# Parallel attention and Mish block: the first root's tiles on two engines, a logarithm behind an eviction, query tiles begun behind scores, two selecting products as one

## Chip, cores and metric

The kernel runs on one core of one Trainium2 chip. The metric is the device time of one execution in microseconds; of several runs the median is given.

## What is computed

A pre-normalised transformer block whose attention and feed-forward halves stand side by side. B = 1, S = 2048 tokens, D = 512, H = 32 heads of Dh = 16, one key head and one value head for all query heads, F = 1792, all in float32:

```python
xn = layernorm(x)                                  # over D, eps = 1e-5
q  = (xn @ wq) as 32 heads;  k = xn @ wk;  v = xn @ wv
p  = softmax(q k^T * Dh ** -0.5)
A  = (p @ v, heads side by side) @ wo
h  = xn @ w1 + b1
Bf = (h * tanh(softplus(h))) @ w2                  # Mish
out = x + A + Bf
```

## The kernel before

Tokens are worked on in four chunks of 512 (`NC`, `CT`), each of four tiles of 128 (`NT`). Engines are called PE (TensorE), DVE (VectorE), ACT (ScalarE), POOL (GpSimd) and SP (DMA issue). The order on every engine is the order in which the code issues; there is no scheduler. Two functions put work off: `later(delay, stage, tag)` queues a step and `run_due` or `flush` issues it. Most products are split into a high and a low fp32r part, with three products in place of one.

There are three sections. The **opening** (to about 97 us) loads the tokens, normalises them, transposes them, forms keys, values and all query tiles, and takes the score maxima of the first unit of four heads. The **hand-ordered section** follows the string `PLAN`, one letter for one step (scores, maxima, exponentials, values, feed-forward products and so on). The **end**, `last_quotient`, divides the last two heads' sums and adds their share of the output projection.

*Normalising a chunk.* `statistics` (L325, L326) takes mean and variance. `rooted` puts variance and negative mean on DVE (L332, L333) and a logarithm and an exponential on ACT (L334, L335) as a first estimate of the reciprocal root. `root` improves it by one step, on POOL or DVE (L339 to L345). `normalise` (L351) applies mean and factor to a token tile on DVE or POOL; `normalise_on_two` leaves the tiles from `n` on to ACT (L359), for which DVE first multiplies factor and mean into a bias (L355). Chunk 0 goes in two halves: the root of tiles 0 and 1 on POOL, that of tiles 2 and 3 on DVE, after which `first_transposes` (L366, evicted by ACT at L368 and DVE at L392) waits for all four tiles. ACT also rounds weight blocks to their high part and POOL subtracts for the low part (`split`, L240, L241).

*Banks.* PSUM has eight banks. Six of them go round as three pairs, taken by `pair_bank` in turn for each step of first maxima (two scores, L495, emptied by one DVE reduction, L512) and for each transpose group of chunks 2 and 3 (L380, emptied by ACT at L382 and L387). While `beside` still holds transposes and key tiles, every query tile uses the same other bank, 7: its twelve products (L708) are followed by an eviction on ACT (L453, and L454 for the high part), and the next tile's first product waits for L453. The key products of a chunk are L417.

*The loop of first maxima.* Steps `i` = 0 to 31 each issue two scores and a reduction. Between them `beside_slot` issues a transpose group or three key products, and `fill_to_end(n)` up to `n` query products; a tile that ends early leaves the rest in `owed`, for the next call. At `i` = 1 the second half of the statistics of chunk 3 and its `rooted` are issued, then a whole query tile.

*The end.* `pick` holds columns of the identity that select, out of the 128 rows of the last value sums `ov`, the 64 sums of exponentials and the 64 weighted sums. Two products (L621, L622) put them in two banks, both at partitions 64 to 127. ACT takes logarithm and exponential of the former (L626, L627), DVE improves and multiplies (L628 to L630), ACT and DVE split the result (L633, L634), and `last_products` (L647) adds the last block of the output projection, for which 18 other products of L647 are the filler before it. L637 adds and L638 stores.

Of the kernel before, what the change touches and what calls it, by code (L numbers as in the profile page):

```python
# [12 lines left out]
ALU = mybir.AluOpType  # L13
# [7 lines left out]
NT = CT // P  # L21
# [157 lines left out]
def attention_and_mlp(ctx: ExitStack, tc: tile.TileContext, x, wq, wk, wv, wo, w1, b1, w2, out):  # L179
    nc = tc.nc  # L180
    E = mybir.EngineType
    PE, SP = nc.tensor, nc.sync
    ACT, DVE, POOL = nc.scalar, nc.vector, nc.gpsimd
# [12 lines left out]
    BANK = [banks[:, i] for i in range(8)]  # L196
# [8 lines left out]
    turn, beside = [0], [None]  # L205
# [32 lines left out]
    def split(hi, lo, src):  # L238

        ACT.activation(hi, src, AF.Copy)  # L240
        POOL.tensor_tensor(out=lo, in0=src, in1=hi.bitcast(F32), op=ALU.subtract)  # L241
# [86 lines left out]
    def rooted(c, some=slice(0, NT)):  # L328
        if c not in ROOT:
            ROOT[c] = [first.tile([P, NT], F32, tag=n, name=f"{n}{c}", bufs=2) for n in ("v", "y", "z", "m")]  # L330
        v, y, z, m = (t[:, some] for t in ROOT[c])
        DVE.tensor_scalar(v, MV[c][:, some, 1], EPS, -0.5, op0=ALU.add, op1=ALU.mult)  # L332
        DVE.tensor_scalar_mul(m, MV[c][:, some, 0], -1.0)  # L333
        ACT.activation(z, v, AF.Ln, scale=-2.0)  # L334
        ACT.activation(y, z, AF.Exp, scale=-0.5)  # L335

    def root(c, engine, some=slice(0, NT)):
        v, y, z, m = (t[:, some] for t in ROOT[c])
        engine.tensor_tensor(out=z, in0=y, in1=y, op=ALU.mult)  # L339
        engine.tensor_tensor(out=z, in0=z, in1=v, op=ALU.mult)  # L340
        if engine is DVE:
            DVE.scalar_tensor_tensor(out=y, in0=z, scalar=1.5, in1=y, op0=ALU.add, op1=ALU.mult)
        else:
            engine.tensor_scalar_add(z, z, 1.5)
            engine.tensor_tensor(out=y, in0=y, in1=z, op=ALU.mult)  # L345

    def normalise(c, engine, some=range(NT)):
        v, y, z, mean = ROOT[c]
        for t in some:
            x, m, r = XS[c, t], mean[:, t : t + 1], y[:, t : t + 1]  # L350
            engine.tensor_scalar(x, x, m, r, op0=ALU.add, op1=ALU.mult)  # L351

    def normalise_on_two(c, n, begin=0):
        v, y, z, mean = ROOT[c]
        DVE.tensor_tensor(out=z[:, n:], in0=y[:, n:], in1=mean[:, n:], op=ALU.mult)  # L355
        normalise(c, DVE, range(begin, n))
        for t in range(n, NT):
            x, b, r = XS[c, t], z[:, t : t + 1], y[:, t : t + 1]
            ACT.activation(x, x, AF.Identity, bias=b, scale=r)  # L359

    def first_transposes():
        xt, FLAT[0] = x_tile(0, work)
        pts = [pair_bank(f"xt0_{k}") for k in range(2)]
        for t in range(NT):
            for d in range(DT):
                PE.transpose(pts[d // 2][:, d % 2, t * P : (t + 1) * P], XS[0, t].rearrange("p (n d) -> p d n", d=DT)[:, d], ident)  # L366
        for d in range(DT):
            ACT.activation(xt[:, 0, d], pts[d // 2][:, d % 2], AF.Copy)  # L368
            if d % 2:
                hi, lo = (xt[:, k, d - 1 : d + 1] for k in range(2))  # L370
                later(0, lambda hi=hi, lo=lo, pt=pts[d // 2]: below(DVE, lo, pt, hi), ("lo", 0))
# [28 lines left out]
    XS, ST, MV, ROOT, FLAT = {}, {}, {}, {}, {}  # L400
# [211 lines left out]
    def last_quotient():  # L612

        c, mt = NC - 1, DT - 1
        rows = slice(64, P)
        pick = late_pool.tile([P, 2, HG * DH], F32, name="pick")
        DVE.tensor_copy(pick.rearrange("p k (h d) -> p k h d", h=HG), ident.rearrange("p (h k d) -> p k h d", h=HG, k=2))
        po, pd = (BANK[4 + k][rows] for k in range(2))
        ov = OV[(NU - 1) % 2]
        last_sums(0, 2)  # L620
        PE.matmul(pd, pick[:, 0], ov, start=True, stop=True)  # L621
        PE.matmul(po, pick[:, 1], ov, start=True, stop=True)  # L622
        last_sums(2, NT)
        hi, lo = (OHL[c, mt][rows, k] for k in range(2))
        o, d, r, z = oc[rows], dc[rows], r0[rows], z0[rows]
        ACT.activation(z, pd, AF.Ln)  # L626
        ACT.activation(r, z, AF.Exp, scale=-1.0)  # L627
        DVE.tensor_tensor(out=d, in0=pd, in1=r, op=ALU.mult)  # L628
        DVE.scalar_tensor_tensor(out=r, in0=d, scalar=2.0, in1=r, op0=ALU.subtract, op1=ALU.mult)
        DVE.scalar_tensor_tensor(out=o, in0=po, scalar=-1.0, in1=r, op0=ALU.mult, op1=ALU.mult)  # L630
        for t in range(NT):
            q = slice(t * P, (t + 1) * P)
            ACT.activation(hi[:, q], o[:, q], AF.Copy)  # L633
            DVE.tensor_tensor(out=lo[:, q], in0=o[:, q], in1=hi[:, q].bitcast(F32), op=ALU.subtract)  # L634
        for t in range(NT):
            last_products(t, mt)
            DVE.tensor_tensor(out=YS[t], in0=BANK[t], in1=YS[t], op=ALU.add)  # L637
            SP.dma_start(out=of[c * CT + t * P : c * CT + (t + 1) * P, :], in_=YS[t])  # L638

    def last_sums(t0, t1):  # L640
        for t in range(t0, t1):
            for mt in range(DT - 1):
                last_products(t, mt)

    def last_products(t, mt):
        for k, (i, j) in enumerate(TERMS):
            PE.matmul(  # L647
                BANK[t],
                OHL[NC - 1, mt][:, i, t * P : (t + 1) * P],
                RG[(blocks_of[NC - 1, "wo"] + mt) % RING][:, j],  # L650
                start=mt == 0 and k == 0,
                stop=mt == DT - 1 and k == 2,
            )
# [69 lines left out]
    done, left = [0], [0]  # L723
# [16 lines left out]
    with tc.tile_pool(name="first", bufs=1) as first:  # L740
# [36 lines left out]
        statistics(0, range(2))  # L777
        rooted(0, halves[0])
        root(0, POOL, halves[0])
        for r in (0, 64):  # L780
            hi, lo = (wkv[:, i, :, r : r + 48].rearrange("p t (k d) -> p t k d", k=3) for i in range(2))
            split(hi, lo, wkv_raw[:, :, None, :DH].to_broadcast([P, DT, 3, DH]))
        statistics(0, range(2, NT))
        rooted(0, halves[1])
        normalise(0, DVE, range(2))
        root(0, DVE, halves[1])
        normalise_on_two(0, 3, 2)
        for r in (0, 64):
            split(wkv[:, 0, :, r + 48 : r + 64], wkv[:, 1, :, r + 48 : r + 64], wkv_raw[:, :, DH:])
# [41 lines left out]
        def beside_slot():  # L831

            while beside:
                if next(beside[0], beside) is not beside:
                    return 3 if len(beside) % 2 else 2
                beside.pop(0)
            return 0

        owed = [0]

        def fill_to_end(n):
            n += owed[0]
            owed[0] = n - fill_slot(n) if done[0] < 12 * (NC * DT + 1) else 0

        def fill_slots(n):
            n, owed[0] = n + owed[0], 0
            while n > 0 and done[0] < 12 * (NC * DT + 1):
                n -= fill_slot(n)
# [3 lines left out]
        for i, (kc, qt, pair) in enumerate(order):  # L852
            now[0] = i // 2 - 100
            first_maxima(kc, qt, pair)
            if i == 1:
                statistics(3, range(2, NT))
                rooted(3)
            if i == 7:
                root(3, POOL)
                normalise(3, POOL)  # L860
            if i == 1:
                fill_slots(12)
            if i % 2 and i > 1:
                if beside:
                    beside_slot()
                    fill_to_end(5 if i < 6 else 3)
                    beside_slot()
                    fill_to_end(4 if i < 6 else 2)
                else:
                    fill_slots(8)  # L870
            run_due(2)
            if i == 22:
                for a in range(2):
                    r = slice(a * 64 + 48, a * 64 + 50)
                    SP.dma_start(out=KS[r].bitcast(F32), in_=ones[:, None].to_broadcast([2, KT, P]))
# [93 lines left out]
    for p in todo + [None]:  # L969
        c, kind, i, t = (NC - 1, "f", 0, 0) if p is None else (p.c, p.kind, p.i, p.t)  # L970
# [74 lines left out]
    for token in word:  # L1045
        k = count.get(token, 0)
# [73 lines left out]
```

## Time and profile before

| | before |
|---|---|
| median of 3 runs | 1548.69 us (1548.55 to 1549.93) |
| profiled execution: time, span | 1549.18 us, 1547.3 us |
| PE, weight loads, DVE, ACT, POOL busy | 99%, 55%, 87%, 87%, 56% |
| granted TensorE clock | 1.00 in every stretch asked for |
| opening, 0 to 57 us: PE busy | 52.2 of 57.0 us |

In a timeline row stand the start in us, the length in us, the engine, the line and operation, output and input, shapes and count; in brackets is the idle time of the engine before it and what ended it. In a list of waits stand who waited for whom, us in total, times, and the longest. Matmul ends are modelled and overlap the next start, so PE work is best timed from start to start. Lines are those of the kernel before.

### The profile page before, as it was taken

The numbers are of one execution on the slowest core, as the hardware profiler recorded it, in microseconds if no ns is written. First come the engines' busy times: TensorE is split into PE (matmuls) and PEld (weight loads), VectorE is DVE, ScalarE is ACT, GpSimd is POOL, SyncE is SP. The second block draws the span as 40 slices with busy tenths as digits, with TensorE's granted clock in tenths as the row PEclk, the third lists the DMA queues.
The fourth block names the chain that finished last, engine by engine and source line by source line (L and its number), as shares of the span: only waits on it lengthen the run. The fifth ranks groups of instructions, "written<-read, shape, count | busy, mean of one in ns | idle before, by whom it ended". The sixth has DMA issues, their size and how long they took to land.

```text
span 1547.3 us, 30218 instructions
## 1 busy us (share of the span) xinstructions
PE 1537.1 (99%) x11544; PEld 844.9 (55%) x11544; DVE 1348.7 (87%) x2285; ACT 1342.8 (87%) x2389; POOL 865.0 (56%) x761
## 2 busy tenths in 40 slices
PE   9999999999999999999999999999999999999998
PEld 7665555555555555545555555555555555555554
DVE  7869998898898898999989999999988998998841
ACT  6569988998999889898889988988898989888896
POOL 6868665675665446544555474733364746353652
PEclk9999999999999999999999999999999999999999
DMA  6773322252123321124322321142222312142120
GB/s 205 294 272 131 107 77 86 74 169 85 58 60 103 104 73 60 52 78 162 80 73 94 114 93 56 43 135 84 86 94 80 99 67 78 33 126 94 43 97 28
DMA packets 69399, 152.53 MB, mean 99 GB/s; under 512 B 12774, under 2 KB 22054, under 8 KB 68870
## 3 DMA queue, kind: packets, MB, share of 16 engines
q1 hardware_dynamic: 69254, 150.60, 29.8%
q8 instruction: 91, 1.49, 0.4%
q14 instruction: 54, 0.44, 0.1%
HBM read 98.51 MB, written 51.64 MB: 97 GB/s over the span
## 4 chain that ended last, share of the span: by engine, by line
PE 97%; DVE 2%; ACT 0%; DMA 0%; issue 0%; SPq 0%; ACTq 0%; DVEq 0%
PE banks L565 33%; PE banks L948 24%; PE banks L561 19%; PE banks L495 18%; PE banks L708 3%; PE banks L647 1%; DVE st L325 0%; PE banks L417 0%; DVE nm L507 0%; DVE X L392 0%; DMA pt<-in_A_x_dram 0%; PE banks L380 0%; DVE pt L351 0%; DVE v L332 0%; DVE ysb L637 0%; DVE nm L512 0%
## 5 line engine op out<-in xcount | busy, mean ns | idle before, releaser
L507 DVE TENSOR_REDUCE nm<-banks 128x1 f32<-128x512 f32 x1984 | 1241.7, 684 | 125.4 <-PE banks L495 71.2
L1013 ACT ACTIVATE pt<-banks 128x512 f32<-128x512 f32 x1590 | 858.3, 604 | 105.0 <-PE banks L561 48.2
L495 PE MATMUL banks<-KS,QS 48*128 48x512 f32 x2048 | 693.4, 421 | 0.0
L561 PE MATMUL banks<-QS,KS 64*128 64x512 f32 x2048 | 681.1, 417 | 0.0
L565 PE MATMUL banks<-pt,V 128*32 128x512 f32 x4096 | 536.2, 603 | 0.0
L561 PEld LDWEIGHTS banks<-QS,KS 64*128 64x128 f32 x2048 | 330.6, 184 | 225.5 <-DVE nm L507 106.8
L495 PEld LDWEIGHTS banks<-KS,QS 48*128 48x128 f32 x2048 | 334.2, 184 | 195.4 <-DVE nm L507 99.8
L948 PE MATMUL banks<-X,wblk 64*128 64x512 f32 x1296 | 330.7, 396 | 0.9 <-DVE nm L507 0.5
L948 PE MATMUL banks<-ring,act 64*128 64x512 f32 x1344 | 328.6, 396 | 0.2
L1005 ACT ACTIVATE pt<-banks 128x1024 f32<-128x1024 f32 x229 | 233.3, 1030 | 34.6 <-PE banks L561 22.6
L948 PEld LDWEIGHTS banks<-X,wblk 64*128 64x128 f32 x1296 | 214.8, 185 | 32.7 <-issue 15.4
L948 PEld LDWEIGHTS banks<-ring,act 64*128 64x128 f32 x1344 | 212.7, 185 | 34.3 <-issue 11.1
L565 PEld LDWEIGHTS banks<-pt,V 128*32 128x32 f32 x4096 | 85.8, 108 | 177.2 <-issue 166.5
L959 POOL TENSOR_TENSOR ysb<-ysb,ty 128x512 f32<-128x512 f32 x80 | 102.9, 1287 | 121.2 <-ACT ty L958 120.7
L688 POOL TENSOR_TENSOR tn<-tn,tr 128x512 f32<-128x512 f32 x54 | 69.5, 1287 | 139.0 <-ACT tr L1023 139.0
L1018 POOL TENSOR_SCALAR tu<-tu 128x512 f32<-128x512 f32 x54 | 80.4, 1488 | 119.5 <-ACT tu L1017 119.1
L241 POOL TENSOR_TENSOR act<-th,act 128x512 fp32r<-128x512 f32 x56 | 72.2, 1291 | 128.0 <-ACT act L240 106.8
L691 POOL TENSOR_TENSOR th<-th,tn 128x512 f32<-128x512 f32 x56 | 72.3, 1292 | 0.0
L1020 POOL TENSOR_TENSOR tn<-tn,tu 128x512 f32<-128x512 f32 x54 | 69.6, 1289 | 4.5
L690 POOL TENSOR_TENSOR tz<-tz,tn 128x512 f32<-128x512 f32 x54 | 69.6, 1289 | 4.5
L692 POOL TENSOR_TENSOR th<-th,tz 128x512 f32<-128x512 f32 x54 | 69.6, 1289 | 4.2
L948 PE MATMUL banks<-ring,ohl 64*128 64x512 f32 x288 | 65.5, 397 | 0.0
(117 smaller groups left out, 960.5 us busy)
## 6 DMA issues: line engine op xcount, KB each, us to landing
wblk<-w_dram SPq DMA_DIRECT2D x42, 512.0 KB
ring<-w_dram SPq DMA_DIRECT2D x42, 512.0 KB
QS<-q_dram SPq DMA_DIRECT2D x62, 192.0 KB
q_dram<-q SPq DMA_DIRECT2D x16, 512.0 KB
o_dram<-ov SPq DMA_DIRECT2D x31, 256.0 KB
raw_w<-in_B_w_dram SPq DMA_DIRECT2D x28, 256.0 KB
w_dram<-wblk SPq DMA_DIRECT2D x14, 512.0 KB
w_dram<-ring SPq DMA_DIRECT2D x14, 512.0 KB
```

Of the source, the lines that this page charges most:

```text
L241: POOL.tensor_tensor(out=lo, in0=src, in1=hi.bitcast(F32), op=ALU.subtract)
L495: PE.matmul(tile, QS[u][rows, pair, qt * P : (qt + 1) * P], KS[rows, kc * CT : (kc + 1) * CT], start=True, stop=True,)
L507: DVE.tensor_reduce(out=m[:, a : a + 1], in_=tile, axis=AX.X, op=ALU.max)
L561: PE.matmul(bank, KS[rows, kt * P : (kt + 1) * P], QS[u][rows, pair], start=True, stop=True)
L565: PE.matmul(BANK[7][h * 32 : (h + 1) * 32], V[:, kt], PT.pop((u * KT + kt) * HG + h), start=kt == 0, stop=kt == KT - 1,)
L690: POOL.tensor_tensor(out=z, in0=z, in1=n, op=ALU.subtract)
L691: POOL.tensor_tensor(out=h, in0=h, in1=n, op=ALU.mult)
L948: PE.matmul(self.p, w[rows], x[rows], start=self.first, stop=not any(self.todo))
L959: POOL.tensor_tensor(out=YS[t], in0=YS[t], in1=ty, op=ALU.add)
L1005: ACT.activation(slots[slot // 2], banks[:, bank : bank + 2], AF.Exp, scale=SCALE)
L1013: ACT.activation(PT[n], BANK[bank], AF.Exp, scale=SCALE)
L1018: POOL.tensor_scalar_min(tu, tu, U_MAX)
```

## The change

Four edits. In the opening, tile 1 of chunk 0 is normalised on ACT in place of DVE, with its bias computed on POOL (`bias`, `normalise_on_act`); `rooted(3)` is issued after the query tile of step 1 in place of before it; and where a query tile has just ended at the end of a step and no transpose or key piece is left half way, the second `fill_to_end` only adds to `owed`. At the end, the two selecting products are one, with sums of exponentials at partitions 0 to 63 and weighted sums at 64 to 127 of one bank.

```diff
+    def bias(c, engine, some):
+        v, y, z, mean = (t[:, some] for t in ROOT[c])
+        engine.tensor_tensor(out=z, in0=y, in1=mean, op=ALU.mult)
+    def normalise_on_act(c, some):
+        v, y, z, mean = ROOT[c]
+        for t in some:
+            x, b, r = XS[c, t], z[:, t : t + 1], y[:, t : t + 1]
+            ACT.activation(x, x, AF.Identity, bias=b, scale=r)
...
         root(0, POOL, halves[0])
+        bias(0, POOL, slice(1, 2))
...
-        normalise(0, DVE, range(2))
+        normalise(0, DVE, range(1))
+        normalise_on_act(0, range(1, 2))
...
             if i == 1:
                 statistics(3, range(2, NT))
-                rooted(3)
...
             if i == 1:
                 fill_slots(12)
+                rooted(3)
...
                     fill_to_end(5 if i < 6 else 3)
+                    at_end = not left[0] and len(beside) % 2 == 0
                     beside_slot()
-                    fill_to_end(4 if i < 6 else 2)
+                    if at_end:
+                        owed[0] += 4 if i < 6 else 2
+                    else:
+                        fill_to_end(4 if i < 6 else 2)
...
-        po, pd = (BANK[4 + k][rows] for k in range(2))
+        pd, po = BANK[4][:64], BANK[4][rows]
...
-        PE.matmul(pd, pick[:, 0], ov, start=True, stop=True)
-        PE.matmul(po, pick[:, 1], ov, start=True, stop=True)
+        PE.matmul(BANK[4], pick.rearrange("p k n -> p (k n)"), ov, start=True, stop=True)
```

What this moves, in the order of the programs. ACT before, where chunk 3's logarithm and exponential (L334, L335) stand, with a query tile's eviction (L453, L454) and chunk 2's transposes (L382, L387):

```order
L240 ACTIVATE wq_127<-th_75 128x256 x2
L334 ACTIVATE z_455<-v_453 128x4
L335 ACTIVATE y_454<-z_455 128x4
L453 ACTIVATE q_1_473<-banks 128x512
L454 ACTIVATE q_1_473<-q_1_473 128x512
L382 ACTIVATE X_486<-banks 128x512
```

The same place of the changed kernel, whose lines are numbered seven higher there (L460 is the eviction, L389 the transposes):

```order
L240 ACTIVATE wq_127<-th_75 128x256 x2
L460 ACTIVATE q_1_466<-banks 128x512
L461 ACTIVATE q_1_466<-q_1_466 128x512
L334 ACTIVATE z_471<-v_469 128x4
L335 ACTIVATE y_470<-z_471 128x4
L389 ACTIVATE X_487<-banks 128x512
```

The eviction now stands ahead of the logarithm; nothing else on ACT changed places there. PE before, from the end of a query tile (wq_121) on, at steps 6 and 7 of the first maxima (L495 scores, L417 keys):

```order
L708 MATMUL banks<-X_231,wq_121 128x512 x3
L380 MATMUL banks<-ident,pt_82 128x128 x2
L380 MATMUL banks<-ident,pt_83 128x128 x2
L708 MATMUL banks<-X_231,wq_127 128x512 x6
L495 MATMUL banks<-KS,QS_88 128x512 x4
L417 MATMUL banks<-X_486,wkv 128x512 x3
L708 MATMUL banks<-X_231,wq_127 128x512 x3
```

PE at that place in the changed kernel (L714 query products, L387 transposes, L502 scores, L424 keys):

```order
L714 MATMUL banks<-X_232,wq_121 128x512 x3
L387 MATMUL banks<-ident,pt_82 128x128 x2
L387 MATMUL banks<-ident,pt_83 128x128 x2
L502 MATMUL banks<-KS,QS_88 128x512 x4
L424 MATMUL banks<-X_487,wkv 128x512 x3
L714 MATMUL banks<-X_232,wq_127 128x512 x9
```

The first six products of the next query tile moved behind four scores and three key products; the same happens once more, at steps 14 and 15, with two products. In all else PE's order is the old one, but for the end, where L621 and L622 are now one product of 128 rows:

```order
L647 MATMUL banks<-ring_1029,ohl_1042 128x512 x3
L621 MATMUL banks<-ov_1052,pick 64x512
L622 MATMUL banks<-ov_1052,pick 64x512
L647 MATMUL banks<-ring_1027,ohl_1040 128x512 x3
L647 MATMUL banks<-ring_1028,ohl_1041 128x512 x3
```

That piece is from before; the changed kernel has, between the same products (L653 there):

```order
L653 MATMUL banks<-ring_1030,ohl_1043 128x512 x3
L628 MATMUL banks<-ov_1053,pick 128x512
L653 MATMUL banks<-ring_1028,ohl_1041 128x512 x3
L653 MATMUL banks<-ring_1029,ohl_1042 128x512 x3
L653 MATMUL banks<-ring_1030,ohl_1043 128x512 x3
```

One instruction is gone from PE and the filler follows it directly. DVE has one operation less (tile 1), ACT and POOL one more each; SP's order is the same.

More of the change, by code (lines that the diff above doesn't have):

```diff
@@ L351, in normalise, with normalise_on_two @@
             engine.tensor_scalar(x, x, m, r, op0=ALU.add, op1=ALU.mult)
-    def normalise_on_two(c, n, begin=0):
+    def bias(c, engine, some):
+        v, y, z, mean = (t[:, some] for t in ROOT[c])
+        engine.tensor_tensor(out=z, in0=y, in1=mean, op=ALU.mult)
+    def normalise_on_act(c, some):
         v, y, z, mean = ROOT[c]
-        DVE.tensor_tensor(out=z[:, n:], in0=y[:, n:], in1=mean[:, n:], op=ALU.mult)
-        normalise(c, DVE, range(begin, n))
-        for t in range(n, NT):
+        for t in some:
             x, b, r = XS[c, t], z[:, t : t + 1], y[:, t : t + 1]
             ACT.activation(x, x, AF.Identity, bias=b, scale=r)
+    def normalise_on_two(c, n, begin=0):
+        bias(c, DVE, slice(n, NT))
+        normalise(c, DVE, range(begin, n))
+        normalise_on_act(c, range(n, NT))
     def first_transposes():
```

## The prediction

> **What bounds the kernel now.** I read the page first: its span and its chain of work that ended last.
>
> ```profile
> span 1547.3 us, 30218 instructions
> ...
> PE 97%; DVE 2%; ACT 0%; DMA 0%; issue 0%; SPq 0%; ACTq 0%; DVEq 0%
> ```
>
> TensorE (PE) is the chain. The table of stretches shows how that looks in the long section whose order is written out by hand (columns: stretch, its length, then busy time of PE, weight loads, VectorE, ScalarE, GpSimd; granted clock, DMA share):
>
> ```profile
> 125.00:1530.00 1405.00, 1404.20 (x10860) 752.83 (x10857) 1245.82 (x2106) 1260.11 (x2237) 776.73 (x666) 1.00 0.27 85
> ```
>
> The change puts no instruction of that section elsewhere, so what PE gains before it is carried through it, if nothing there hangs on an absolute time. PE's waits over the whole run are few:
>
> ```profile
> PE banks L708 <- ACT q L453: 2.3, 3, 1.4
> ...
> PE banks L366 <- DVE pt L351: 0.6, 2, 0.3
> ```
>
> Both are in the first 60 us and both are what the opening edits aim at. So each edit is worth what PE stops waiting there, less what it then waits for instead; the last edit is worth PE time at the very end. For both I read the timelines, engine by engine (start us, length, engine, line).
>
> **Opening, first root.** Of chunk 0's four token tiles, VectorE normalised three and ScalarE one; now it is two and two, and GpSimd computes one more small bias.
>
> ```profile
> 7.51 1.28 DVE L351 TENSOR_SCALAR pt<-pt,m,y 128x512 f32<-128x512 f32 x2
> ...
> 9.48 0.81 ACT L359 ACTIVATE pt<-pt,z,y 128x512 f32<-128x512 f32 x1 [1.49 <-DVE z L355]
> ...
> 6.75 0.20 POOL L345 TENSOR_TENSOR y<-y,z 128x2 f32<-128x2 f32 x1
> 6.90 1.15 POOL L241 TENSOR_TENSOR wkv<-wkv_raw,wkv 128x192 fp32r<-128x192 f32 x2
> ```
>
> VectorE sheds half of 1.28 us, about 0.6. ScalarE had idled 1.49 us, so tile 1 costs it nothing; tiles 2 and 3 and the transposes behind them come up to 0.6 us earlier. The bias is a GpSimd operation like that of 6.75 (0.20 us): it moves the weight split behind it by 0.2 to 0.3 us and could hold VectorE up by as much, so the gain is 0.2 to 0.6 us at 11 us. It does not last. ScalarE next waits for DMAs that no computation starts:
>
> ```profile
> 14.52 0.63 ACT L240 ACTIVATE wblk<-raw_w 128x512 fp32r<-128x512 f32 x1 [1.07 <-DMA raw_w<-in_B_w_dram]
> ...
> 15.23 1.30 POOL L241 TENSOR_TENSOR wblk<-raw_w,wblk 128x512 fp32r<-128x512 f32 x1 [0.41 <-ACT wblk L240]
> ...
> 15.99 0.56 DVE L332 TENSOR_SCALAR v<-mv 128x4 f32<-128x4 f32 x1
> ...
> 22.34 0.75 ACT L240 ACTIVATE wq<-tn 128x256 fp32r<-128x256 f32 x2 [1.63 <-DMA tn<-in_A_wq_dram]
> ...
> 23.55 1.94 ACT L382 ACTIVATE X<-banks 128x1024 fp32r<-128x1024 f32 x2
> ...
> 24.60 2.36 DVE L392 TENSOR_TENSOR X<-banks,X 128x1024 fp32r<-128x1024 f32 x2 [1.06 <-ACT X L382]
> ```
>
> The split at 14.52 and with it GpSimd's 15.23 stay. L332 lasts 0.56 us and ends at 16.55, when GpSimd's operation ends at 16.53: issued 0.2 to 0.6 us sooner (15.4 to 15.8, after 15.23 still) it ends at the same time. At 22.34 ScalarE waits for a DMA again, in front of L382, on which VectorE's 24.60 hangs. From there VectorE has its old times. I take 0 for this edit (between 0 and 0.6; below nothing is excluded, since the transposes can lose at most 0.3 us and the same DMA waits swallow that).
>
> The Trainium skill has a rule here: "SBUF — State Buffer", section "SBUF: two separate sides", says that VectorE's faster modes and GpSimd share one pair of ports, which the first to start holds for its whole instruction. By that rule L332 cannot finish before GpSimd does, the first root's gain stays 0, and the rival below in which it lasts becomes less likely; the trace agrees, with 16.55 against 16.53.
>
> **Opening, last chunk's logarithm.** The logarithm stood on ScalarE's queue ahead of a query tile's eviction, and PE waited for that eviction:
>
> ```profile
> 32.08 2.59 POOL L392 TENSOR_TENSOR KS<-kvs,KS 16x512 fp32r<-16x512 f32 x2
> ...
> 32.54 0.83 DVE L332 TENSOR_SCALAR v<-mv 128x4 f32<-128x4 f32 x1
> ...
> 33.40 0.20 ACT L334 ACTIVATE z<-v 128x4 f32<-128x4 f32 x1 [3.58 <-DVE v L332]
> ...
> 33.75 0.58 ACT L453 ACTIVATE q<-banks 128x512 f32<-128x512 f32 x1
> ...
> 28.66 3.01 PE L708 MATMUL banks<-X,wq 128*128 128x512 f32 x12
> ...
> 32.27 0.75 PE L380 MATMUL banks<-ident,pt 128*128 128x128 f32 x4
> 34.38 1.43 PE L708 MATMUL banks<-X,wq 128*128 128x512 f32 x5 [1.37 <-ACT q L453]
> 35.65 0.63 PE L380 MATMUL banks<-ident,pt 128*128 128x128 f32 x4
> ```
>
> The tile is done at 28.66 + 3.01 = 31.67. With L453 first, its bank is free by about 32.3, before PE gets there at 33.0: the 1.37 us go. The logarithm itself still starts at 33.4 (L332 ends at 33.37, with GpSimd's first half of 2.59 us), and the evictions behind it on ScalarE keep their times, so nobody is newly late by it. What is late next is the transpose group of 35.65. It would come at 34.28, but three pairs of banks go round, and its pair is emptied by the first of these two reductions:
>
> ```profile
> 33.35 2.35 DVE L512 TENSOR_REDUCE nm<-banks 128x2 f32<-128x1024 f32 x2
> ```
>
> Maxima steps 2 and 3 and transposes 0 and 1 take the pairs 2, 0, 1 and 2. The first reduction ends half way, at about 34.55, and PE goes on at 34.6. The edit gains 35.65 - 34.6 = 1.05 us (bounds 1.05 and 1.37).
>
> **Opening, query tiles begun behind scores.** Where a query tile has just ended, the next no longer begins at once in the same bank; the score products go first. Twice:
>
> ```profile
> 37.14 0.73 PE L495 MATMUL banks<-KS,QS 48*128 48x512 f32 x4
> ...
> 39.09 0.63 PE L380 MATMUL banks<-ident,pt 128*128 128x128 f32 x4
> 40.22 1.66 PE L708 MATMUL banks<-X,wq 128*128 128x512 f32 x6 [0.49 <-ACT q L453]
> ...
> 37.68 2.36 DVE L512 TENSOR_REDUCE nm<-banks 128x2 f32<-128x1024 f32 x2 [1.98 <-PE banks L495]
> ...
> 52.62 2.36 DVE L512 TENSOR_REDUCE nm<-banks 128x2 f32<-128x1024 f32 x2 [0.61 <-PE banks L495]
> ...
> 54.16 0.63 PE L380 MATMUL banks<-ident,pt 128*128 128x128 f32 x4
> ...
> 55.28 0.73 PE L708 MATMUL banks<-X,wq 128*128 128x512 f32 x2 [0.49 <-ACT q L453]
> ```
>
> The 0.49 us waits go, but the scores have a wait of their own: their pair is the one that the second reduction empties, at 37.68 + 2.36 = 40.04 and 52.62 + 2.36 = 54.98. PE goes on at 40.1 in place of 40.22 and at 55.03 in place of 55.28. (VectorE had idled before both reductions, so they move with PE.) That is 0.12 + 0.25 = 0.37 us, between 0 and 0.98; a loss is excluded because the same products follow in either order.
>
> **End, both selecting products as one.** Two products of 64 columns each become one of 128 columns:
>
> ```profile
> 1534.06 1.07 PE L621 MATMUL banks<-ov,pick 128*64 128x512 f32 x2
> 1534.97 1.02 PE L622 MATMUL banks<-ov,pick 128*64 128x512 f32 x2
> 1535.92 7.14 PE L647 MATMUL banks<-ring,ohl 128*128 128x512 f32 x30
> ...
> 1527.05 2.78 PE L565 MATMUL banks<-pt,V 128*32 128x512 f32 x24
> ...
> 1538.86 0.91 ACT L633 ACTIVATE ohl<-oc 64x128 fp32r<-64x128 f32 x4 [2.44 <-DVE oc L630]
> ...
> 1539.20 0.91 DVE L634 TENSOR_TENSOR ohl<-oc,ohl 64x128 fp32r<-64x128 f32 x4 [0.37 <-ACT ohl L633]
> ```
>
> A 64-column product takes 0.91 to 0.95 us, start to start. One of 128 columns isn't in the trace: as long as one (gain 0.93) or as long as two (gain 0). L565 decides: 24 records are 12 products of 32 columns, four of them side by side, 2.78 / 3 = 0.93 us for four, so fewer columns are not faster, and I take 0.93. The logarithm and division start when they did. PE's 18 products of filler (7.14 / 30 = 0.238 us each) then end at 1534.99 + 4.28 = 1539.27. The last block needs its high part from 1539.1 and, two products later at 1539.75, the low part, there at 1539.20 + 0.25 = 1539.45. PE stays the bound by 0.3 us and the output moves by the full 0.93.
>
> **Sum.** 0 + 1.05 + 0.37 + 0.93 = 2.35 us off the profiled execution's 1549.18 is 1546.83; that one was 0.49 over the median, so 1548.69 - 2.35 = 1546.3. With the bounds of the terms (gain 1.4 to 3.3) this case by itself spans 1545.4 to 1547.3. A measurement tells some 0.2% (3.1 us) from no change: faster is below 1545.6, slower above 1551.8. By this sum the change is real but under that.
>
> **Rivals.**
> *All the waits go* (0.24): if the DMAs of 14.52 and 22.34 or the reductions don't hold the opening, it keeps 0.6 + 1.37 + 0.98, with 0.93 at the end 3.88 us: 1544.8. For it: the list of waits charges PE's time to L453 alone. Against it: 33.35 and 40.04 above.
>
> *Only the end counts* (0.10): the opening's gain is given back to transfers.
>
> ```profile
> 87.20 0.60 ACT L453 ACTIVATE q<-banks 128x512 f32<-128x512 f32 x1 [2.49 <-DMA q_dram<-q]
> ...
> 82.00:84.00 2.00, 2.00 (x10) 1.63 (x9) 1.72 (x7) 1.05 (x2) 2.00 (x3) 1.00 0.00 0
> ```
>
> Evictions from 87 us wait for query stores. If those keep their time, PE runs into full banks and only 0.93 is left: 1547.8. Against it: the DMA share is 0.00 at 82 to 84 us, so the stores start when computation lets them, and move along.
>
> *Slower* (0.06): the hand-ordered section falls into another rhythm.
>
> ```profile
> PEld banks L561 <- DVE nm L507: 106.8, 139, 0.8
> ```
>
> Its weight loads already wait 106.8 us for VectorE; if such waits grew onto PE's path by 6% of that (6.4 us), the 2.35 us would be gone and 4.0 us more: 1552.7. It decides from 2.35 us on. Against it: the order is unchanged and all engines enter it shifted alike.
>
> That the change doesn't do what it says has no chance: the order of instructions shows each move.
>
> **Numbers.** Forecast 0.60, rivals 0.24, 0.10, 0.06. Predicted: 1546.3. The range reaches from the first rival to the second, 1544.8 to 1547.9. Faster: 0.24 and 0.05 of the forecast's upper bounds, 0.29; slower 0.06; same 0.65.
>
> **What would show it.** In the profile after: no wait of PE for L453, PE waiting for VectorE's first-maxima reductions instead, near 34.6 and 39 us; VectorE's reduction of 33.35 at its old time; the group of 35.65 1.05 us earlier and that of 55.28 about 1.4; one selecting product of 0.9 to 1.0 us. I am wrong if that product takes 1.8, if the reduction moves, or if the first product of the hand-ordered section is not 1.4 us earlier.

## The result, and the profile after

| | before | changed |
|---|---|---|
| median | 1549.48 us (18 runs, 1548.55 to 1552.60) | 1547.22 us (18 runs, 1545.55 to 1549.75) |
| profiled execution: time, span | 1549.18, 1547.3 us | 1546.73, 1545.0 us |

The ratio is 0.9983, with a 95% interval of 0.9976 to 0.9991: by the medians 2.3 us are gone. That is less than the 0.2% which the prediction asks for before it calls a kernel faster, but the interval leaves out 1, so the gain is real. Three single runs of the experiments below stand far out, 3627.34 us with the first edit alone (not in its ratio), 1565.50 with the second alone and 1562.33 with the later statistics (both in theirs, so that these two ratios lie above what the medians give). The page of the changed kernel, its span and the chain that ended last:

```profile
span 1545.0 us, 30216 instructions
...
PE 98%; SPq 1%; DMA 0%; DVE 0%; issue 0%; ACT 0%; DVEq 0%
```

TensorE is still the chain. The list of waits (who waited for whom; us in total, times, longest) has lost its line for L453:

```profile
PE banks L502 <- DVE nm L519: 0.6, 2, 0.4
```

For the opening I compare the starts of groups. Four rows of before that were not shown yet, all of them scores: steps 2 and 3, steps 8 and 9, steps 16 and 17, and the first product of the hand-ordered section:

```profile
31.61 0.73 PE L495 MATMUL banks<-KS,QS 48*128 48x512 f32 x4
...
45.22 0.73 PE L495 MATMUL banks<-KS,QS 48*128 48x512 f32 x4
...
59.34 0.73 PE L495 MATMUL banks<-KS,QS 48*128 48x512 f32 x4
...
96.76 0.50 PE L495 MATMUL banks<-KS,QS 48*128 48x512 f32 x1
```

The same stretches of the changed kernel, TensorE and one row of its weight loads (PEld), with the bracket for an idle time and what ended it:

```profile
32.35 0.73 PE L502 MATMUL banks<-KS,QS 48*128 48x512 f32 x4
33.02 0.75 PE L387 MATMUL banks<-ident,pt 128*128 128x128 f32 x4
33.52 1.41 PE L714 MATMUL banks<-X,wq 128*128 128x512 f32 x5
34.82 0.75 PE L387 MATMUL banks<-ident,pt 128*128 128x128 f32 x4
34.82 0.56 PEld L387 LDWEIGHTS banks<-ident,pt 128*128 128x128 f32 x4 [0.32 <-DVE nm L519]
...
36.44 0.73 PE L502 MATMUL banks<-KS,QS 48*128 48x512 f32 x4
...
38.39 0.63 PE L387 MATMUL banks<-ident,pt 128*128 128x128 f32 x4
39.39 0.73 PE L502 MATMUL banks<-KS,QS 48*128 48x512 f32 x4 [0.37 <-DVE nm L519]
...
44.17 0.73 PE L502 MATMUL banks<-KS,QS 48*128 48x512 f32 x4
...
52.89 0.63 PE L387 MATMUL banks<-ident,pt 128*128 128x128 f32 x4
53.77 0.73 PE L502 MATMUL banks<-KS,QS 48*128 48x512 f32 x4 [0.25 <-DVE nm L519]
...
57.65 0.73 PE L502 MATMUL banks<-KS,QS 48*128 48x512 f32 x4
...
95.05 0.50 PE L502 MATMUL banks<-KS,QS 48*128 48x512 f32 x1
```

From the scores of steps 2 and 3 to the next scores it was 37.14 - 31.61 = 5.53 us and is now 36.44 - 32.35 = 4.09. TensorE shows no wait there, but the weight loads of the transposes at 34.82 still waited 0.32 us for VectorE's first-maxima reduction. From the transposes ahead of the second place to the scores behind it, 45.22 - 39.09 = 6.13 became 44.17 - 38.39 = 5.78; at the third, 59.34 - 54.16 = 5.18 became 57.65 - 52.89 = 4.76. Over the whole way from the scores of steps 4 and 5 to those of steps 16 and 17, 59.34 - 37.14 = 22.20 became 57.65 - 36.44 = 21.21, 0.99 less. The hand-ordered section begins 1.71 us earlier, although steps 2 and 3 come 0.74 later than before (1.44 + 0.99 - 0.74 = 1.69). At the end, the selecting product and VectorE's last additions:

```profile
1532.39 1.02 PE L628 MATMUL banks<-ov,pick 128*128 128x512 f32 x2
...
1538.45 2.82 DVE L643 TENSOR_TENSOR ysb<-banks,ysb 128x512 f32<-128x512 f32 x4
```

These are 6.06 us apart. Before, the additions began at 1541.06, 7.00 us behind the first selecting product. From the product to the end of the span it is 12.6 in place of 13.2 us. The opening (1.71), the hand-ordered section (1437.34 against 1437.30) and the end (0.63) add up to the 2.3 us of the spans.

### The profile page after: what moved, and what is told of

Same layout as the page of the kernel before. It is cut to its first block, busy times and chain, and to the rows that moved or that the text cites. A ratio compares the mean times of both kernels' runs of the same rounds, so it can differ in the third digit from the quotient of the medians.

```text
span 1545.0 us, 30216 instructions
## 1 busy us (share of the span) xinstructions
PE 1537.0 (99%) x11542; PEld 847.6 (55%) x11542; DVE 1347.8 (87%) x2284; ACT 1342.8 (87%) x2390; POOL 864.2 (56%) x762
## 3 DMA queue, kind: packets, MB, share of 16 engines
q8 instruction: 91, 1.49, 0.4%
## 4 chain that ended last, share of the span: by engine, by line
PE 98%; SPq 1%; DMA 0%; DVE 0%; issue 0%; ACT 0%; DVEq 0%
PE banks L572 33%; PE banks L960 23%; PE banks L568 19%; PE banks L502 18%; PE banks L714 3%; PE banks L424 1%; PE banks L653 1%; DMA tn<-in_A_wq_dram 0%; SPq L260 0%; SPq L317 0%; DVE nm L519 0%; DVE ysb L643 0%; PE banks L387 0%; SPq L758 0%; SPq L750 0%
## 5 line engine op out<-in xcount | busy, mean ns | idle before, releaser
L502 PE MATMUL banks<-KS,QS 48*128 48x512 f32 x2048 | 694.6, 421 | 0.7 <-DVE nm L519 0.6
L502 PEld LDWEIGHTS banks<-KS,QS 48*128 48x128 f32 x2048 | 334.4, 185 | 195.7 <-DVE nm L514 99.8
```

The costliest lines, as they stand in the source:

```text
L502: PE.matmul(tile, QS[u][rows, pair, qt * P : (qt + 1) * P], KS[rows, kc * CT : (kc + 1) * CT], start=True, stop=True,)
```

## Experiments: each edit alone

All four ran on one chip beside 35 runs of the kernel before (median 1549.89). Call the edits A (first root), B (logarithm), C (query tiles), D (selecting product).

**A alone.** Tile 1 of chunk 0 goes to ScalarE:

```diff
+        bias(0, POOL, slice(1, 2))
-        normalise(0, DVE, range(2))
+        normalise(0, DVE, range(1))
+        normalise_on_act(0, range(1, 2))
```

> The kernel before with the first edit alone: tile 1 of the first chunk on ScalarE, its bias on GpSimd. Theory (the DMA waits on ScalarE in front of the weight splits hold the opening): the first transposes of tiles 2 and 3 come 0.2 to 0.6 us earlier measured from the arrival of the tokens, the score group that starts at 62.76 us before does not move by more than the transfers themselves do (within 0.3 us), time 0 us. Rival (all the waits go): that score group 0.6 us earlier, time 0.6 us lower.

Measured: 1550.17 us, ratio 1.0000 (0.9991 to 1.0009). First transposes and key product, then ScalarE's wait for a load and, in the weight loads, what held the key products:

```profile
8.99 2.13 PE L373 MATMUL banks<-ident,pt 128*128 128x128 f32 x16
11.45 0.73 PE L424 MATMUL banks<-X,wkv 128*128 128x512 f32 x2 [0.33 <-ACT X L375]
...
22.71 0.74 ACT L240 ACTIVATE wq<-tn 128x256 fp32r<-128x256 f32 x2 [1.42 <-DMA tn<-in_A_wq_dram]
...
27.37 0.30 PEld L424 LDWEIGHTS banks<-X,wkv 128*128 128x128 f32 x2 [0.21 <-DVE X L399]
```

The first key product follows 2.46 us behind the first transposes in place of 3.13 (8.39 to 11.52 before): 0.67 us are gained at 11 us. ScalarE then waits for the weights as predicted, its evictions of chunk 1's transposes are late, VectorE's L399 behind them too, and the key products wait for that. Steps 2 and 3 come at 32.29, not earlier than the 31.99 to 32.02 of the other three. The group of 62.76 comes at 63.33, 0.57 us later; the weights that ScalarE waited for were 0.37 later themselves (22.34 to 22.71).

**B alone.** The logarithm goes behind the query tile of step 1:

```diff
             if i == 1:
                 statistics(3, range(2, NT))
-                rooted(3)
...
                 fill_slots(12)
+                rooted(3)
```

> The kernel before with the second edit alone: the last chunk's logarithm behind the query eviction. Theory: PE's wait of 1.37 us for the eviction is gone and the transpose group after it waits for the first reduction of steps 2 and 3 or comes later anyway; from the score group of steps 2 and 3 to the score group of steps 4 and 5 (31.61 to 37.14 before, 5.53 us) it takes 4.1 to 4.5 us; time 1.05 us lower (0.7 to 1.4). Rival (all the waits go): 4.16 us there, and 1.37 us lower whatever the reductions do.

Measured: 1548.36 us, ratio 0.9999 (0.9981 to 1.0018). The transposes now wait for VectorE, whose reduction starts behind L332:

```profile
32.98 0.96 DVE L332 TENSOR_SCALAR v<-mv 128x4 f32<-128x4 f32 x1
...
33.92 2.34 DVE L512 TENSOR_REDUCE nm<-banks 128x2 f32<-128x1024 f32 x2
...
35.19 0.75 PE L380 MATMUL banks<-ident,pt 128*128 128x128 f32 x4 [0.60 <-DVE nm L512]
```

The new wait is the one forecast, but longer. From scores to scores it is 4.78 us (32.02 to 36.80): 0.75 gained, and not within the 4.1 to 4.5 expected.

**C alone.** The second call only adds to what is owed:

```diff
+                    at_end = not left[0] and len(beside) % 2 == 0
                     beside_slot()
-                    fill_to_end(4 if i < 6 else 2)
+                    if at_end:
+                        owed[0] += 4 if i < 6 else 2
+                    else:
+                        fill_to_end(4 if i < 6 else 2)
```

> The kernel before with the third edit alone: query tiles begun behind the scores. By the prediction's sum: two waits of 0.49 us replaced by waits for VectorE that are 0.12 and 0.25 us shorter, time 0.37 us lower. By what the profile after suggests (merging the query products saves PE about 0.2 us each time besides): from transpose group 39.09 to score group 45.22 (6.13 us before) 5.8 us, from 54.16 to 59.34 (5.18 us) 4.75 us, time 0.8 us lower. Rival (all the waits go): 0.98 us lower with no wait for VectorE.

Measured: 1548.42 us, ratio 0.9992 (0.9984 to 1.0001).

```profile
37.54 0.73 PE L495 MATMUL banks<-KS,QS 48*128 48x512 f32 x4
...
40.49 0.74 PE L495 MATMUL banks<-KS,QS 48*128 48x512 f32 x4 [0.37 <-DVE nm L512]
...
54.88 0.74 PE L495 MATMUL banks<-KS,QS 48*128 48x512 f32 x4 [0.26 <-DVE nm L512]
...
58.76 0.73 PE L495 MATMUL banks<-KS,QS 48*128 48x512 f32 x4
```

The scores wait for the second reduction at both places, as forecast. The stretches take 5.78 and 4.77 us instead of 6.13 and 5.18: 0.76 gained, twice the forecast 0.37. That is not all. From the scores of steps 4 and 5 to those of steps 16 and 17 it takes 58.76 - 37.54 = 21.22 us instead of 22.20, so C is worth 0.98. The other 0.22 lie between the two places, at a transpose group whose order is the same. Its weight loads, before and with C:

```profile
50.94 0.56 PEld L380 LDWEIGHTS banks<-ident,pt 128*128 128x128 f32 x4 [0.38 <-DVE nm L512]
...
50.77 0.57 PEld L380 LDWEIGHTS banks<-ident,pt 128*128 128x128 f32 x4
```

Before, they waited for a reduction; with C they don't, and the scores around them stand 51.93 - 48.94 = 2.99 us apart instead of 52.08 - 48.88 = 3.20. VectorE's reduction began there 0.57 us behind its scores (49.51) and before 0.84 (49.72).

**D alone.**

```diff
-        PE.matmul(pd, pick[:, 0], ov, start=True, stop=True)
-        PE.matmul(po, pick[:, 1], ov, start=True, stop=True)
+        PE.matmul(BANK[4], pick.rearrange("p k n -> p (k n)"), ov, start=True, stop=True)
```

> The kernel before with the fourth edit alone: one selecting product of 128 columns. Theory: it takes 0.86 to 0.95 us as each of the two did, PE stays the bound up to the last block, from its start to the first final addition on VectorE it takes 6.06 us in place of 7.00; time 0.93 us lower. Rival (twice as many columns take twice as long): 7.0 us there and no gain. Second rival (the division now comes too late): PE waits before its last block.

Measured: 1548.79 us, ratio 0.9988 (0.9979 to 0.9996).

```profile
1534.99 1.02 PE L621 MATMUL banks<-ov,pick 128*128 128x512 f32 x2
...
1541.06 2.83 DVE L636 TENSOR_TENSOR ysb<-banks,ysb 128x512 f32<-128x512 f32 x4
```

6.07 us in place of 7.00: the 0.93 of the forecast. One product of 128 columns takes as long as one of 64.

## Experiments: what B and C are worth, and why

The next four ran on one chip (before: 1549.49).

**Is C's surplus a merged group of products?** In C the new tile's six products join three others. Here they stay apart, behind the scores:

```diff
             if i % 2 and i > 1:
                 if beside:
+                    fill_to_end(0)
                     beside_slot()
```

> The changed kernel, but at both places the owed query products follow the scores at once and the key products come behind them, so that the query products stand in two groups (six and three, two and three) instead of one. Waits should be those of the changed kernel. Theory: about half of edit C's gain was one change of operands on TensorE fewer at each place, about 0.2 us each: transposes to next scores 5.95 to 6.0 us (5.78 in the changed kernel) and 4.95 to 5.0 (4.76), all of it kept at the first hand-ordered product. Rival: the whole gain came from waits, some of which the trace rounds away: 5.78 and 4.76 stay within 0.05.

Measured: 1546.83 us, ratio 0.9983 (0.9974 to 0.9991). TensorE at the second place; VectorE and GpSimd at steps 2 and 3:

```profile
38.42 0.74 PE L502 MATMUL banks<-KS,QS 48*128 48x512 f32 x4 [0.36 <-DVE nm L519]
39.09 1.67 PE L714 MATMUL banks<-X,wq 128*128 128x512 f32 x6
...
43.24 0.73 PE L502 MATMUL banks<-KS,QS 48*128 48x512 f32 x4
...
32.45 0.17 DVE L332 TENSOR_SCALAR v<-mv 128x4 f32<-128x4 f32 x1
...
32.53 2.66 POOL L399 TENSOR_TENSOR KS<-kvs,KS 16x512 fp32r<-16x512 f32 x2
```

From the transposes to the scores behind the place it is 5.81 and 4.75 us: my theory falls, merging is worth nothing. What remains is where the stop stands. Up to the first product behind the wait, the change gains 0.13 (40.22 - 39.09 = 1.13 against 39.39 - 38.39 = 1.00), where 0.12 was forecast. The other 0.2 come behind the wait: 5.00 us of the same products before (40.22 to 45.22), 4.78 and 4.82 now. That a stop directly ahead of scores costs less, since the weight loads there are not hidden anyway (they start with the product itself, at 43.24 for one), would fit, but no run isolates it.

This execution shows something else. L332 took 0.17 us, and TensorE shows no wait for the reductions (31.52 to 35.47, 3.95 us).

**Do the statistics hold the reductions?** The second half of chunk 3's statistics, and all behind it, two steps later:

```diff
-            if i == 1:
+            if i == 3:
                 statistics(3, range(2, NT))
...
                 fill_slots(12)
-                rooted(3)
...
+            if i == 3:
+                rooted(3)
             run_due(2)
```

> The changed kernel, but VectorE takes the second half of chunk 3's statistics two maxima steps later, and the logarithm follows the transposes of that step. Theory (edit B fell short because the reductions of steps 2 and 3 wait on VectorE behind these statistics): from the scores of steps 2 and 3 to those of steps 4 and 5 TensorE needs 4.1 us with no wait for VectorE between, where the logarithm edit alone took 4.78 with a wait of 0.60; the reductions begin about 0.9 us after the scores. The statistics then lie ahead of the reductions of steps 4 and 5, so that the wait of 0.37 us in front of the next scores grows to about 0.6. Net gain on the changed kernel 0 to 0.4 us. Rival (the transposes are held by something else): 4.7 us again, and a loss of 0.2 to 0.5 us through the later wait.

Measured: 1547.38 us, ratio 0.9991 (0.9974 to 1.0009).

```profile
35.41 0.73 PE L502 MATMUL banks<-KS,QS 48*128 48x512 f32 x4
...
38.18 0.75 PE L387 MATMUL banks<-ident,pt 128*128 128x128 f32 x4 [0.66 <-DVE nm L519]
...
39.31 0.73 PE L502 MATMUL banks<-KS,QS 48*128 48x512 f32 x4 [0.38 <-DVE nm L519]
```

From 31.50 to 35.41 it is 3.91 us with no wait, as expected. But steps 4 and 5 now pay 0.66 us in a new place (expected: some 0.25). The wait has only moved two steps on.

**Is A lost behind ScalarE's wait for a load?** The rounding of two weight blocks goes behind the evictions of chunk 1:

```diff
-        flush(("wq", 1), ("wq", 2))
...
         run(transposes(1))
+        flush(("wq", 1), ("wq", 2))
```

> The changed kernel, but ScalarE rounds the two query weight blocks of 22.23 us behind its evictions of chunk 1's transposes instead of ahead of them, so that these no longer stand behind a wait for a DMA. Theory (the first root's gain of 0.6 us is lost there): the evictions begin about 1.5 us earlier, the wait of 0.31 us for them goes, and the first scores come 0.3 to 0.6 us earlier relative to the first transposes. Rival (the copies of the query rows or the maxima reductions hold the opening as well): no more than 0.1 us is left at the scores of steps 6 and 7.

Measured: 1547.12 us, ratio 0.9984 (0.9975 to 0.9993).

```profile
21.34 1.99 ACT L389 ACTIVATE X<-banks 128x1024 fp32r<-128x1024 f32 x2 [0.27 <-PE banks L387]
...
32.32 2.62 POOL L399 TENSOR_TENSOR KS<-kvs,KS 16x512 fp32r<-16x512 f32 x2
...
32.43 1.21 DVE L332 TENSOR_SCALAR v<-mv 128x4 f32<-128x4 f32 x1
...
31.51 0.73 PE L502 MATMUL banks<-KS,QS 48*128 48x512 f32 x4
```

The evictions begin 2.9 us earlier than in the changed kernel's profile (24.22) and the wait for them is gone; steps 2 and 3 come 20.09 us behind the first key product (11.42) in place of 20.97. Before it was 20.09 too (11.52 to 31.61), and the first kernel of the next section, which has A and rounds the weights at the old place, takes 31.26 - 11.31 = 19.95: 20.97 is not a matter of the order. And what was won went again at once: GpSimd's split began 0.11 us ahead of L332, which took 1.21 us, and scores to scores took 4.98 us with a wait of 0.80. The scores of steps 6 and 7 come at 39.45, against 39.39 in the changed kernel: nothing is left, as the expectation's rival has it.

**The change without A.**

```diff
-        bias(0, POOL, slice(1, 2))
-        normalise(0, DVE, range(1))
-        normalise_on_act(0, range(1, 2))
+        normalise(0, DVE, range(2))
```

> The changed kernel without its first edit: tile 1 of chunk 0 stays on VectorE. Theory (that edit is worth 0): first transposes to first key product 3.1 us instead of 2.5, but the same time within 0.2 us from the score group near 61 us on, and the same total. Rival (it keeps 0.3 us or more in company with the other edits): the group near 61 us and the first hand-ordered product come 0.3 to 0.6 us later than in the changed kernel.

Measured: 1547.02 us, ratio 0.9981 (0.9972 to 0.9989), as good as with A. The group near 61 us comes at 60.77, 0.29 ahead of the changed kernel's, a little more than the 0.2 expected, and the first key product follows 2.74 us behind the first transposes, not 3.1. TensorE at its first key product, and at the transposes of step 3:

```profile
11.53 0.73 PE L417 MATMUL banks<-X,wkv 128*128 128x512 f32 x2 [0.33 <-ACT X L368]
...
34.53 0.75 PE L380 MATMUL banks<-ident,pt 128*128 128x128 f32 x4 [0.53 <-DVE nm L512]
```

## Experiments: taking the collision away

If L332 beside GpSimd's split is what sets B's price, putting L332 behind the reductions, and leaving the statistics in place, must give B's full price every time. The last three ran on one chip (before: 1549.69).

**The change with `rooted(3)` behind step 3.**

```diff
                 fill_slots(12)
-                rooted(3)
...
+            if i == 3:
+                rooted(3)
             run_due(2)
```

> The changed kernel, but chunk 3's variance and mean copies (L332, L333) and its logarithm are issued behind the two maxima reductions and transposes of steps 2 and 3; the statistics stay where they are. Theory (edit B's gain depends on whether the variance copy, in front of the reductions, falls beside GpSimd's split of the keys and stretches from 0.17 to as much as 1.2 us): the reduction begins 0.9 to 1.1 us behind the scores of steps 2 and 3 in every execution, TensorE waits nowhere between these scores and those of steps 4 and 5 and needs 3.9 to 4.0 us for them, and the later waits stay 0.37 and 0.25; the group near 61 us comes 0 to 1.0 us earlier than in the changed kernel and its siblings, the total the same within what can be told. Rival (the statistics themselves are what holds the reductions): 4.5 us or more with a wait of 0.5 us left.

Measured: 1546.11 us, ratio 0.9975 (0.9965 to 0.9985).

```profile
31.26 0.73 PE L502 MATMUL banks<-KS,QS 48*128 48x512 f32 x4
...
35.16 0.73 PE L502 MATMUL banks<-KS,QS 48*128 48x512 f32 x4
...
32.06 2.33 DVE L519 TENSOR_REDUCE nm<-banks 128x2 f32<-128x1024 f32 x2
```

3.90 us and no wait; the reductions begin 0.80 us behind the scores. The hand-ordered section begins at 93.76 us, 1.29 before that of the changed kernel. Of this, 1.09 us lie ahead of the scores of steps 2 and 3 (31.26 against 32.35), where the edit moves nothing; its own are 4.09 - 3.90 = 0.19.

**The kernel before with this place of `rooted(3)` alone.** The same edit on before's code:

```diff
             if i == 1:
                 statistics(3, range(2, NT))
-                rooted(3)
...
+            if i == 3:
+                rooted(3)
             run_due(2)
```

> The kernel before with nothing changed but the place of chunk 3's variance and mean copies and logarithm: behind the reductions and transposes of steps 2 and 3. Theory: edit B's full price, no wait for the eviction and none for the reduction, 3.9 to 4.0 us from the scores of steps 2 and 3 to those of steps 4 and 5 against 5.53 before, so 1.6 us: the 1.37 us of the wait and about 0.2 us of weight loads that a stopped TensorE leaves uncovered when it starts again. The total 1.5 us shorter. Rival (the price is the 1.37 us alone, as the prediction had it): 4.15 us.

Measured: 1547.92 us, ratio 0.9990 (0.9981 to 0.9999).

```profile
31.60 0.73 PE L495 MATMUL banks<-KS,QS 48*128 48x512 f32 x4
...
35.51 0.73 PE L495 MATMUL banks<-KS,QS 48*128 48x512 f32 x4
```

3.91 us against 5.53: without the collision the edit is worth 1.62, more than the 1.37 in the bracket. That L332 is out of the queue ahead of the reductions would be a rival to the collision, but where it ran unhindered in that place scores to scores took 3.95 us: 0.05 at most. The bracket counts from the modelled end of the last product before the wait, 33.02; unhindered, the next product starts at 0.50 to 0.51 us behind the transposes' start, not at 0.75. From start to start the wait of before cost 34.38 - 32.27 = 2.11 less 0.51, which is 1.60.

**The bias load behind the tokens, too.**

```diff
-            if f == 0:
-                SP.dma_start(out=b1s, in_=b1_column)
...
         load_tokens(3)
+        SP.dma_start(out=b1s, in_=b1_column)
```

> As the first kernel of this call, with the load of the feed-forward bias (a column of 14 numbers per partition) issued behind the loads of chunk 3 instead of between the first weight blocks. Theory (its issue took 0.6 to 1.4 us and moved every later load in step with it): the loads behind it start 0.6 to 1.4 us earlier; the first scores come no earlier if TensorE, which waits nowhere from the first key product on, is the bound there: 0 to 0.3 us, the total like that of the first kernel. Rival (the loads hold the opening): 0.5 us or more off the group near 61 us.

Measured: 1544.72 us (5 runs), ratio 0.9968 (0.9955 to 0.9980).

```profile
span 1542.5 us, 30217 instructions
...
59.88 0.73 PE L502 MATMUL banks<-KS,QS 48*128 48x512 f32 x4
```

The group near 61 us comes at 59.88, in the kernel without this edit at 59.78: no gain in the opening, as expected, although the tokens of chunk 2 are loaded from 8.31 us on in place of 12.46, far more than the 0.6 to 1.4 expected. The five runs lie 1.1 us below the eight with `rooted(3)` alone in the mean, the profiled ones only 0.3 (1544.42 and 1544.71); where a gain would come from no trace shows, so it stays open. Against before it is the shortest version that was run, 0.32%.

Side by side, what each profile shows at this place (us; GpSimd's key split is two halves of 1.3 each):

| kernel | key split begins | L332 begins, lasts | reductions begin | wait of the transposes | scores to scores |
|---|---|---|---|---|---|
| B alone | 32.63 | 32.98, 0.96 | 33.92 | 0.60 | 4.78 |
| without A | 31.97 | 32.40, 0.88 | 33.26 | 0.53 | 4.72 |
| weights rounded later | 32.32 | 32.43, 1.21 | 33.62 | 0.80 | 4.98 |
| changed kernel | 32.27 | 33.27, 0.30 | 33.55 | none (weight loads 0.32) | 4.09 |
| six and three apart | 32.53 | 32.45, 0.17 | 32.60 | none (weight loads 0.20) | 3.95 |
| `rooted(3)` later | 31.80 | 34.30, 0.16 | 32.06 | none | 3.90 |

In the first four L332 ends when the split's first half does (32.63 + 1.27 = 33.90, for one, against 32.98 + 0.96 = 33.94). The same holds, to within 0.04 us, in the profiles of before and of A, C and D alone. In the fifth L332 started 0.08 us ahead of the split and went through.

## Why the prediction was right, and which steps were not

Forecast were 2.35 us; the profiled executions differ by 2.45, the medians by 2.26. The median came out 0.9 us above the 1546.3, of which 0.8 is that of before: 1549.48 in 18 runs, where the first three of them had given 1548.69. By the time alone 1547.22 lies nearer the 1547.8 of "only the end counts" than 1546.3; it is the traces that rule this rival out, and the others with it. But the sum held by luck. In the profiled pair the terms are -0.74 ahead of steps 2 and 3, 1.44, 0.99 and 0.63, together 2.32, where 0, 1.05, 0.37 and 0.93 were forecast: two terms came out 1.01 larger, and late loads and the tail took 1.04 away. What the terms were in the executions without a profile, no run shows.

- **First root, 0 (bounds 0 to 0.6).** Right in size: the change without it takes the same time. Half right in its reason. The load in front of L382 took the gain back in the executions with late loads: steps 2 and 3 follow the first key product by 20.84 us in the A kernel and by 20.97 in the changed kernel's profile. In four others with A and in all six without it they follow by 19.9 to 20.1, so some tenths then remain, too small for the totals. (In the run with later statistics it is 20.29, and why is open.) That all three long ones have A may be more than chance: the issue of the bias column took 0.62 to 0.64 us in the six profiles without A and 0.62 to 1.46 in the six that have A and load it at the same place. No run isolates this.
- **Logarithm, 1.05 (1.05 to 1.37).** The step that failed is "L332 ends at 33.37, with GpSimd's first half", taken as a fixed time. It is a race between VectorE and GpSimd that went differently in profiles of kernels which issue these operations alike. (One profile was taken of each kernel.) Lost, the edit gives 0.55 to 0.81 us (5.53 less 4.98 to 4.72); won, 1.58; in the changed kernel's profile 1.44. Both bounds were too narrow. The lower one, because GpSimd's split and TensorE do not keep a fixed distance, and because transposes that had to stop take 1.60 to 1.62 us to the next scores (35.19 to 36.80, for one) instead of the 1.49 of before. The upper one, because the bracket of 1.37 is 1.60 from start to start. The wait that was named as next, VectorE's first-maxima reduction, is there in three of the executions, as the table shows. In the profile after, TensorE came late itself, and only 0.32 us of it are left, in the weight loads; that is what keeps 4.09 above 3.90.
- **Query tiles, 0.37 (0 to 0.98).** Both waits are where they were said to be, 0.37 and 0.25 us long. The term was far too small: it measured 0.98, at the upper bound, though not because the waits went. Of the 0.61 that were left out, 0.22 are a wait of the weight loads between the two places. The other 0.4 come behind the two stops (5.00 us became 4.78, and 4.06 became 3.88); that a stop costs less in front of scores than in front of six or two query products would fit, and stays argued. Merged groups, my first explanation, are excluded.
- **End, 0.93.** Right: 0.93 and 0.94 from the product to the last additions. From the product to the end of the span it is about 0.8 (13.2 to 13.4 us without the edit, 12.4 to 12.6 with it), as the output's tail grew a little. The prediction had taken the end of the span to move by the full 0.93.
- **The rival "all the waits go"** did not come for the change, but with `rooted(3)` behind step 3 the gain is about as large as its 3.88: 3.58 and 4.97 us against before on the same chip (1546.11 and 1544.72).
- **"Slower" and "only the end counts"** can be ruled out: the hand-ordered section took 1437.34 us, as before (1437.30), and began 1.71 us earlier.
- **The signs.** The wait for L453 is gone, two waits for the reductions stand at 39.39 and 53.77, and the selecting product is one. But the wait near 34.6 is not in TensorE's list, the reduction of 33.35 began at 33.55, the group of 35.65 came 0.83 earlier instead of 1.05, and the hand-ordered section 1.71 instead of 1.4.
- **The range.** The bounds of the four terms add up to a gain of 2.0 to 3.9 us (1.05 if the selecting product had gained nothing), not 1.4 to 3.3. The range given does not hang on them, since it reaches from rival to rival.

## What to carry to other kernels

Price a wait from start to start against the same pair of groups where it doesn't occur, not by its bracket: here 1.37 us in brackets were 1.60. Before moving a long operation off a wait, look at the short ones queued ahead of the next releaser: a copy of 128x4 numbers that falls beside a GpSimd operation can take 1.2 us in place of 0.17, and putting it behind the reductions made a gain of 0.55 to 1.58 us into 1.62. Look at the weight loads too: waits of 0.2 to 0.4 us stood there and not in TensorE's list. And terms that miss can still give a right sum, so run the parts by themselves and measure each over a stretch long enough to hold all that it moves.

## What was not expected of the hardware

- **A race of a tenth of a microsecond sets a microsecond.** VectorE's L332 took 0.17 us when it began 0.08 us ahead of GpSimd's split, and 1.21 when it began 0.11 us behind. The Trainium skill, "SBUF — State Buffer", section "SBUF: two separate sides", has the rule: VectorE in a faster mode and GpSimd share a port pair, which the first to start holds to the end of its instruction. The trace agrees where GpSimd came first: L332 then ended with GpSimd's operation, to within 0.04 us, in eight profiles. Where VectorE came first, L332 kept its 0.17 us, which fits; which mode it ran in no trace shows.
- **The order is the same, the time is not.** From its first product to the selecting product the hand-ordered section took 1436.2 to 1438.9 us in the thirteen profiled executions, whose kernels issue it alike. In eight of them TensorE waited 0.2 to 1.4 us for weight blocks. That is as large as the whole change, and why the totals of single edits say little where the traces say much.
- **A small load can hold a queue.** The bias column's issue took 0.62 us in the profile of before and 1.41 in that of the changed kernel, and the loads behind it began 0.7 to 1.0 us later. The issue right behind it is dearer still: it took 3.1 to 4.1 us in all thirteen profiles. In the last kernel, where the column stands elsewhere, it is another weight block, which took 0.55 to 1.15 in the other twelve. The opening gained nothing from moving it.
